# Two gates ahead of two values, and one output step fewer ahead of the first score burst: a change at the batch boundaries of an attention and gated feed-forward kernel

## The chip, the core and the metric

The kernel runs on one core of one Trainium2 chip. The metric is the device time of one execution in microseconds (us). The engines are named as the profile names them: PE (TensorE matmul), PEld (TensorE weight load), DVE (VectorE), ACT (ScalarE), POOL (GpSimd). The clock that PE was granted was 1.0 in the profiled executions.

## The reference, cut to what matters

```python
# 8 batches, 8 heads, 576 tokens, 16 beacon keys, head size 64
scores = scale * q @ k_all.T          # causal, the 16 beacon keys seen by all
a = softmax(scores)
x = (a @ v_all) as [4608 tokens, 512]
out = (gelu(x @ w_gate) * (x @ w_val)) @ w_out     # 512 -> 1536 -> 512
```

## The kernel before: the parts concerned

The feed-forward part runs in nine chunks of 512 tokens. For chunk b there are 12 gate/value tiles; each needs four gate matmuls, four value matmuls, a gelu on ACT and a product on DVE. The output matmuls of chunk b are delayed into batch b + 1, where they fill PE while ACT computes exponentials (at the boundary of batches 2 and 3 from 126.11 to 128.06 us, with exponentials on ACT from 125.97 on): a score burst fills one of three score buffers, and the exponential empties it. At each boundary the program has ACT load the function table for exp, 1.28 us in the trace, between the last gelu and the first exponential. Names with `psum` are the program's buffers for PE's results; a bank here is room for one 128x512 f32 tile. A half-height matmul is one that the profile shows as 64\*128 (a full one is 128\*128), and an output step of the first output tile is two of them side by side: in the trace of the kernel before, the two start 0.004 us apart (125.051 and 125.055) and the next step 0.216 us later (125.267).

```python
psum_s = ...bufs=3   # three buffers of two PSUM banks: scores, gate+value tiles, attention outputs
psum_t = ...bufs=1   # one bank
psum_o = ...bufs=1   # one bank

def gv_mms(ci, fi, *kks, split=False, last=False):
    # split: gate tile g_ps in psum_t, value tile v_ps in psum_s[:, 0]; else both in one psum_s buffer
    ...
    part(0)                       # the gate matmuls
    if not split: part(1)         # the value matmuls
    ...
    act(ge_sb, gv_of[ci, fi][0], ACT.Gelu)
    if split: part(1)
    ...
    keep(nc.vector.tensor_tensor(out=h_of[ci][:, fi, :], in0=gv_of.pop((ci, fi))[1], in1=ge_sb, op=ALU.mult))

def out_half_mms(ci, u0, u1):     # first output tile: two half-height matmuls side by side, one bank each
    for fi in range(u0, u1):
        if fi == 0:
            o_of[ci] = [..., (out_ps(0), out_ps(1))]          # psum_t and psum_o
        for g in range(2):
            r = slice(64 * g, 64 * g + 64)
            mm(halves[g], h_of[ci][r, fi, 0:P], wo_sb[r, fi, :], fi == 0, fi == F_TILES - 1, ...)
        if fi == F_TILES - 1:
            out_store(ci, 0, halves[0], o_half=halves[1])

def out_store(ci, ti, o_ps, c0=0, c1=D_MODEL, o_half=None):
    ...
        keep(nc.vector.tensor_copy(o_ap, o_half))                            # empties psum_o
        keep(nc.vector.tensor_tensor(out=o_ap, in0=o_ps, in1=o_ap, op=ALU.add))
    ...

for b in range(B):
    if b:
        keep(nc.scalar.preload_act_table_set(SET_EXP))
        o(3, b > 1)                       # b > 1: half height
        scores(b, (0, 0))                 # first burst: three buffers
        scores(b, (0, 2))
        scores(b, (0, 1))
        o(5 if b == 1 else 9, b > 1)      # the twelfth step ends the first output tile
        ...
        scores(b, (0, 3), (1, 3))         # fourth
        scores(b, (1, 0))
        scores(b, (1, 2))                 # needs the buffer of (0, 1): waits for the third exponential
        ...
        o(5 if b == 1 else 6)             # second output tile, full height, in psum_o
        ...
    for fi in range(F_TILES):
        if fi >= 2:
            gate_val(b, fi, fi == F_TILES - 1 and b < B - 1)
```

I count the score steps as the text does: (0, 0), (0, 2), (0, 1) are the first, second and third; (0, 3) with (1, 3) the fourth; (1, 0); and (1, 2), which the prediction calls the fifth burst.

The softmax here doesn't subtract the row's maximum and nothing guards it: scores larger than these inputs give would overflow.

## Time and profile before

| | before |
|---|---|
| median of 3 runs | 365.84 us |
| span of the profiled execution | 364.1 us |
| PE, ACT, DVE busy | 97%, 53%, 45% |
| one batch (start of the last product of a batch to the next) | 38.950 us, five times |
| PE's waits for exponentials | 0.9 us, 6 times |

The batch length is read from the trace as the distance between the starts of the DVE products that end each batch: 86.05 us for batch 1 and 280.80 for batch 6, so (280.80 - 86.05) / 5 = 38.95. The page's chain of waits by engine says which engines the end of the kernel hangs on:

```profile
span 364.1 us, 7726 instructions
PE 80%; DMA 8%; POOL 6%; ACT 3%; issue 2%; DVE 0%; ACTq 0%; POOLq 0%
```

The reader is to see ACT with 3%: the only engine besides PE that the chain meets in the steady batches. (DMA and POOL come in through the start-up: the chain's pieces from 80 to 174 us hold none of either.)

### The profile page before, as it was taken

Reading aid. Unit: us, or ns where it says so; the run is one execution under the profiler, and the core shown is the slowest. Engines: PE = TensorE matmul, PEld = TensorE weight load, DVE = VectorE, ACT = ScalarE, POOL = GpSimd, SP = SyncE. Lnnn points to the kernel's source line nnn. Section 1 sums busy time; section 2 is a strip of 40 time slices with the busy share of each in tenths; the row PEclk is TensorE's granted clock in tenths of the full one; section 3 lists DMA queues with packets and bytes.
Section 4 is the critical chain, followed back from the end, with each engine's and each line's share of the span. In section 5 each row is a group of like instructions: output and inputs, shape, how many; then the busy total and the mean of one; then the engine's idle time right before and its main releaser. Section 6 shows DMA issues by size and latency. Waiting matters only on the chain.

```text
span 364.1 us, 7726 instructions
## 1 busy us (share of the span) xinstructions
PE 353.7 (97%) x3164; PEld 184.8 (51%) x3206; DVE 162.8 (45%) x320; ACT 192.7 (53%) x252; POOL 161.2 (44%) x288
## 2 busy tenths in 40 slices
PE   7899999999999999999999999999999999999996
PEld 6665446444654455445644464446544564444443
DVE  4547836344443345434534354334444453333332
ACT  3975788237923594349623891379335953321210
POOL 8934497655537552945375455565330530000000
DMA  7999999899179945999299917991797253000102
GB/s 105 173 203 204 198 126 99 129 170 188 23 126 147 215 45 76 163 215 64 56 148 221 111 38 121 170 198 27 112 136 136 17 60 115 0 2 29 58 36 110
DMA packets 160419, 41.57 MB, mean 114 GB/s; under 512 B 146944, under 2 KB 155904, under 8 KB 160384
## 3 DMA queue, kind: packets, MB, share of 16 engines
q0 software_dynamic: 104848, 19.11, 68.9%
q1 hardware_dynamic: 55536, 21.96, 30.7%
q8 instruction: 25, 0.41, 0.5%
q14 instruction: 10, 0.08, 0.1%
HBM read 38.27 MB, written 9.44 MB: 131 GB/s over the span
## 4 chain that ended last, share of the span: by engine, by line
PE 80%; DMA 8%; POOL 6%; ACT 3%; issue 2%; DVE 0%; ACTq 0%; POOLq 0%
PE gv_ps L168 42%; PE o_ps L168 21%; PE x_ps L168 8%; PE s_ps L168 6%; DMA wo_sb<-in_moe_w_out_dram 4%; DMA qk<-in_q_dram 4%; ACT expT L171 3%; POOL qk L111 1%; PE g_ps L168 1%; PE v_ps L168 1%; POOL v_sb L111 1%; POOL q_sb L111 1%; POOL wg_sb L111 1%; POOL wv_sb L111 1%; POOL expT L320 1%
## 5 line engine op out<-in xcount | busy, mean ns | idle before, releaser
L171 ACT ACTIVATE ge_sb<-gv_ps 128x512 bf16<-128x512 f32 x101 | 59.4, 597 | 141.8 <-PE gv_ps L168 139.5
L448 DVE TENSOR_TENSOR hT_sb<-gv_ps,ge_sb 128x512 bf16<-128x512 f32 x101 | 69.0, 691 | 111.6 <-ACT ge_sb L171 109.2
L168 PE MATMUL gv_ps<-xT_sb,wg_sb 128*128 128x512 bf16 x402 | 111.2, 379 | 0.5
L168 PE MATMUL gv_ps<-xT_sb,wv_sb 128*128 128x512 bf16 x388 | 107.9, 379 | 0.4
L171 ACT ACTIVATE expT<-s_ps 128x992 bf16<-128x992 f32 (+3 forms) x112 | 100.2, 979 | 7.0 <-PE s_ps L168 6.4
L168 PE MATMUL o_ps<-wo_sb,hT_sb 128*128 128x512 bf16 (+3 forms) x492 | 101.0, 373 | 1.3
L320 POOL TENSOR_SCALAR_AFFINE_SELECT expT<-expT 128x256 bf16<-128x256 bf16 (+1 forms) x140 | 52.2, 391 | 51.2 <-ACT expT L171 50.0
L168 PEld LDWEIGHTS <-wv_sb 128*128 128x128 bf16 x432 | 42.3, 98 | 50.6
L168 PEld LDWEIGHTS <-wg_sb 128*128 128x128 bf16 x432 | 42.1, 98 | 49.9
L168 PEld LDWEIGHTS <-hT_sb 128*128 128x128 bf16 (+1 forms) x516 | 39.5, 97 | 42.4 <-issue 4.1
L168 PEld LDWEIGHTS <-expT 128*128 128x128 bf16 (+1 forms) x960 | 33.6, 97 | 10.0 <-DVE y_sb L356 3.1
L168 PE MATMUL x_ps<-v_sb,expT 128*128 128x65 bf16 (+1 forms) x960 | 37.4, 193 | 0.2 <-POOL expT L320 0.2
L168 PE MATMUL s_ps<-qkT 64*128 64x80 bf16 (+5 forms) x528 | 33.6, 250 | 3.4 <-DVE qkT L239 1.6
L111 POOL DMA_DIRECT2D v_sb<-in_v_dram x40 | 33.6, 859 | 6.0 <-DMA wg_sb<-in_moe_w_gate_dram 1.8
L111 POOL DMA_DIRECT2D k_sb<-in_k_dram x30 | 25.2, 844 | 15.4 <-DMA q_sb<-in_q_dram 10.8
L356 DVE TENSOR_TENSOR y_sb<-x_ps,r_sb 128x320 bf16<-128x320 f32 (+1 forms) x47 | 28.8, 612 | 1.6
L111 POOL DMA_DIRECT2D q_sb<-in_q_dram x30 | 25.3, 879 | 6.4 <-DMA wo_sb<-in_moe_w_out_dram 3.5
L469 DVE COPY o_sb<-o_ps 128x512 f32<-128x512 f32 (+2 forms) x31 | 20.7, 668 | 15.3 <-PE o_ps L168 14.2
L354 DVE RECIPROCAL r_sb<-x_ps 128x5 f32<-128x5 f32 (+1 forms) x47 | 9.6, 204 | 39.1 <-PE x_ps L168 39.1
L168 PEld LDWEIGHTS <-qkT 64*128 64x128 bf16 x528 | 18.1, 95 | 17.2 <-issue 8.9
L399 POOL COPY hold_sb<-xT_sb 128x2 bf16<-128x2 bf16 x6 | 1.1, 186 | 30.8 <-DMA xT_sb<-y_sb 30.8
L471 DVE COPY o_sb<-o_ps 128x512 f32<-128x512 f32 x6 | 4.1, 691 | 15.4 <-PE o_ps L168 15.4
(58 smaller groups left out, 137.9 us busy)
## 6 DMA issues: line engine op xcount, KB each, us to landing
out_dram<-o_sb SPq DMA_DIRECT2D x35, 256.0 KB, 7.0
v_sb<-in_v_dram POOLq DMA_DIRECT2D x24, 128.0 KB, 9.0
q_sb<-in_q_dram POOLq DMA_DIRECT2D x18, 128.0 KB, 12.2
k_sb<-in_k_dram POOLq DMA_DIRECT2D x18, 128.0 KB, 5.8
wo_sb<-in_moe_w_out_dram POOLq DMA_DIRECT2D x3, 512.0 KB, 14.4
wg_sb<-in_moe_w_gate_dram POOLq DMA_DIRECT2D x2, 512.0 KB, 11.9
wv_sb<-in_moe_w_val_dram POOLq DMA_DIRECT2D x2, 512.0 KB, 13.5
v_sb<-in_v_dram POOLq DMA_DIRECT2D x8, 112.0 KB, 5.4
```

What stands on the lines that cost most here:

```text
L111: keep(nc.gpsimd.dma_start(out=out_ap, in_=in_ap))
L168: keep(nc.tensor.matmul(out_ap, lhsT, rhs, start=start, stop=stop, **kw))
L171: keep(nc.scalar.activation(out_ap, in_ap, func, **kw))
L320: nc.gpsimd.affine_select(out=d, in_=d, pattern=[[0, 2], [1, n]], compare_op=ALU.is_ge, fill=0.0, base=0, channel_multiplier=-1,)
L354: keep(nc.vector.reciprocal(r, x[:, :, :, D:DV]))
L356: nc.vector.tensor_tensor(out=y_of[i][:, :, h0:h1, :].rearrange("p j b d -> p b j d"), in0=x[:, :, :, 0:D], in1=r.to_broadcast([P, h1 - h0 ...
L399: keep(nc.gpsimd.tensor_copy(hold_sb, x[:, 0 : S : S - 1]))
L448: nc.vector.tensor_tensor(out=h_of[ci][:, fi, :], in0=gv_of.pop((ci, fi))[1], in1=ge_sb, op=ALU.mult)
L469: keep(nc.vector.tensor_copy(o_ap, o_ps))
L471: keep(nc.vector.tensor_copy(o_ap, o_half))
```

## The change

Its intent: bring the first exponential of a batch forward. The last gelu, and so the table load, is to come earlier because both gates of the last two tiles run before both values; the first scores are to come earlier because one output step moves from before the first burst to after it.

```diff
+    def gates_first(ci, *fis):
+        ge_of = {}
+        for fi, (pool, tag) in zip(fis, ((psum_t, "t"), (psum_o, "o"))):
+            g_ps = pool.tile([P, CH], FP32, name="g_ps", tag=tag)
+            part(ci, fi, 0, g_ps)
+            ge_of[fi] = gelu(g_ps)
+        for fi in fis:
+            v_ps = psum_s.tile([P, 2, CH], FP32, name="v_ps", tag="s")[:, 0, :]
+            part(ci, fi, 1, v_ps)
+            gated(ci, fi, v_ps, ge_of[fi])
 ...
-            o(3, b > 1)
+            o(3 if b == 1 else 2, b > 1)
             scores(b, (0, 0))
             scores(b, (0, 2))
             scores(b, (0, 1))
-            o(5 if b == 1 else 9, b > 1)
+            o(5 if b == 1 else 10, b > 1)
 ...
         for fi in range(F_TILES):
-            if fi >= 2:
-                gate_val(b, fi, fi == F_TILES - 1 and b < B - 1)
+            if fi >= 2 and (fi < F_TILES - 2 or b in (0, B - 1)):
+                gate_val(b, fi, b == 0 and fi == F_TILES - 1)
+            if fi == F_TILES - 2 and 0 < b < B - 1:
+                gates_first(b, fi, fi + 1)
```

The rest of the diff (cut) only takes the old helper apart into `part`, `gelu` and `gated`.

More of the change, by code (lines that the diff above doesn't have):

```diff
@@ L411, with part @@
     gv_of = {}
-    def gv_mms(ci, fi, *kks, split=False, last=False):
-        if (ci, fi) not in gv_of:
-            if split:
-                gv_of[ci, fi] = (
-                    psum_t.tile([P, CH], FP32, name="g_ps", tag="t"),
-                    psum_s.tile([P, 2, CH], FP32, name="v_ps", tag="s")[:, 0, :],
-                )
-            else:
-                gv_ps = psum_s.tile([P, 2, CH], FP32, name="gv_ps", tag="s")
-                gv_of[ci, fi] = (gv_ps[:, 0, :], gv_ps[:, 1, :])
-        n0 = ci * CH
-        def part(w):
-            for kk in kks:
-                mm(
-                    gv_of[ci, fi][w],
-                    (wg_sb, wv_sb)[w][:, kk, fi * P : (fi + 1) * P],
-                    xT_sb[:, kk, n0 : n0 + CH],
-                    kk == 0,
-                    last and kk == kks[-1],
-                    skip_group_check=True,
-                )
-        part(0)
-        if not split:
-            part(1)
-        if not last:
-            return
+    def part(ci, fi, w, ps, kks=range(K_CHUNKS), last=True):
+        n0 = ci * CH
+        for kk in kks:
+            mm(
+                ps,
+                (wg_sb, wv_sb)[w][:, kk, fi * P : (fi + 1) * P],
+                xT_sb[:, kk, n0 : n0 + CH],
+                kk == 0,
+                last and kk == kks[-1],
+                skip_group_check=True,
+            )
@@ L441, in gv_mms, with gelu, gated @@
+    def gelu(g_ps):
         ge_sb = fpool.tile([P, CH], BF16, name="ge_sb", tag="ge_sb")
-        act(ge_sb, gv_of[ci, fi][0], ACT.Gelu)
-        if split:
-            part(1)
+        act(ge_sb, g_ps, ACT.Gelu)
+        return ge_sb
+    def gated(ci, fi, v_ps, ge_sb):
         if ci not in h_of:
             h_of[ci] = hpool.tile([P, F_TILES, CH], BF16, name="hT_sb", tag="hT_sb")
-        keep(
-            nc.vector.tensor_tensor(
-                out=h_of[ci][:, fi, :], in0=gv_of.pop((ci, fi))[1], in1=ge_sb, op=ALU.mult
-            )
-        )
@@ L453, in gate_val, with gv_mms @@
-    def gate_val(ci, fi, split=False):
-        gv_mms(ci, fi, *range(K_CHUNKS), split=split, last=True)
+        keep(nc.vector.tensor_tensor(out=h_of[ci][:, fi, :], in0=v_ps, in1=ge_sb, op=ALU.mult))
+    def gv_mms(ci, fi, *kks, last=False):
+        if (ci, fi) not in gv_of:
+            gv_of[ci, fi] = psum_s.tile([P, 2, CH], FP32, name="gv_ps", tag="s")
+        gv_ps = gv_of[ci, fi]
+        for w in range(2):
+            part(ci, fi, w, gv_ps[:, w, :], kks, last)
+        if last:
+            gated(ci, fi, gv_ps[:, 1, :], gelu(gv_ps[:, 0, :]))
@@ new lines, in gate_val @@
+    def gate_val(ci, fi, split=False):
+        if not split:
+            gv_mms(ci, fi, *range(K_CHUNKS), last=True)
+            return
+        g_ps = psum_t.tile([P, CH], FP32, name="g_ps", tag="t")
+        v_ps = psum_s.tile([P, 2, CH], FP32, name="v_ps", tag="s")[:, 0, :]
+        part(ci, fi, 0, g_ps)
+        ge_sb = gelu(g_ps)
+        part(ci, fi, 1, v_ps)
+        gated(ci, fi, v_ps, ge_sb)
+    def gates_first(ci, *fis):
+        ge_of = {}
+        for fi, (pool, tag) in zip(fis, ((psum_t, "t"), (psum_o, "o"))):
+            g_ps = pool.tile([P, CH], FP32, name="g_ps", tag=tag)
+            part(ci, fi, 0, g_ps)
+            ge_of[fi] = gelu(g_ps)
+        for fi in fis:
+            v_ps = psum_s.tile([P, 2, CH], FP32, name="v_ps", tag="s")[:, 0, :]
+            part(ci, fi, 1, v_ps)
+            gated(ci, fi, v_ps, ge_of[fi])
```

## The prediction

What the trace of the kernel before shows at this boundary, for the terms that the prediction uses:

- Matmuls of 512 columns follow one another after 0.216 us, while most of their records last 0.376 to 0.379 us, so a gap between records understates a stall. That fewer columns take less in proportion is an estimate that the trace bears out to 0.01 us: the next matmul starts 0.162 us after one of 384 columns (125.699 to 125.861; 0.162 in proportion), and the two 208-column chunks take 0.183 us (128.056 to 128.239; 0.176).
- The table load takes 1.283 us, and the first exponential starts 0.011 us after its end (125.964 to 125.975). An event semaphore stands ahead of that exponential (125.902) and another ahead of the last product (124.934).
- From half height to full height the next matmul starts 0.094 us later than that pace (128.987 due, 129.081), and from full to half 0.096 (124.729 due, 124.825).

> **What bounds the kernel now.** I read the page first: the engine shares, then the waits of the tensor engine, then the chain of waits, then the timeline of one batch boundary engine by engine. The shares and the wait list:
>
> ```profile
> PE 353.7 (97%) x3164; PEld 184.8 (51%) x3206; DVE 162.8 (45%) x320; ACT 192.7 (53%) x252; POOL 161.2 (44%) x288
> PE s_ps L168 <- ACT expT L171: 0.9, 6, 0.2
> ```
>
> PE is busy 97% of 364.1 us and every other engine about half. After the start-up the wait list of PE has one repeated entry: six waits, 0.9 us in all, of score matmuls for an exponential. The change touches six batch boundaries (batches 1 to 6 into 2 to 7), so these six waits are its target. The windows view agrees that each batch is a copy of the last: 38.95 us per batch, PE busy 38.52 in each of five windows. The chain of waits at the boundary of batches 2 and 3:
>
> ```profile
> 124.89 0.76 PE o_ps L168 x6
> 125.65 0.65 PE s_ps L168 x14
> 126.30 0.02 issue
> 126.32 0.02 ACTq L171
> 126.33 0.56 issue
> 126.89 1.84 ACT expT L171 x2
> 128.73 0.04 issue
> 128.78 0.37 PE s_ps L168 x4
> ```
>
> The reader is to see that the chain, on PE everywhere else in a batch, crosses over to ACT here for 2.4 us and comes back at 128.78. The timeline of the same stretch:
>
> ```profile
> 124.07 0.60 ACT L171 ACTIVATE ge_sb<-g_ps 128x512 bf16<-128x512 f32 x1 [0.27 <-PE g_ps L168]
> 124.68 1.28 ACT L616 ACT_TABLE_LOAD   x1
> 125.00 0.69 DVE L448 TENSOR_TENSOR hT_sb<-v_ps,ge_sb 128x512 bf16<-128x512 f32 x1 [0.48 <-PE v_ps L168]
> 125.48 0.80 PE L168 MATMUL s_ps<-qkT 64*128 64x512 bf16 x14
> 126.11 2.11 PE L168 MATMUL o_ps<-wo_sb,hT_sb 64*128 64x512 bf16 x18
> 127.72 1.00 ACT L171 ACTIVATE expT<-s_ps 128x992 bf16<-128x992 f32 x1
> 128.06 0.56 PE L168 MATMUL s_ps<-qkT 64*128 64x128 bf16 x10
> 128.26 0.69 DVE L471 COPY o_sb<-o_ps 128x512 f32<-128x512 f32 x1 [2.57 <-PE o_ps L168]
> 128.78 0.37 PE L168 MATMUL s_ps<-qkT 64*128 64x384 bf16 x4 [0.16 <-ACT expT L171]
> ```
>
> The last gelu ends at 124.67, the table load for the exponential at 125.96, the first exponential starts at 125.97, the third ends at 127.72 + 1.00 = 128.72 and frees the score buffer that the fifth burst (head pair 1, chunk 2) needs: it starts at 128.78. Then o matmuls of full height go on at 129.08.
>
> **How long PE really stands still.** The 0.16 us shown is measured from the end of a 0.38 us record, but four such matmuls in a row span 1.03 us, so one starts every (1.03 - 0.38) / 3 = 0.216 us. The second burst group began at 128.06 with two 208-column chunks (416/512 x 0.216 = 0.18) and one of 512 (0.216); the fifth burst could have started at 128.45. PE loses 128.78 - 128.45 = **0.32 us** per boundary, six times: 1.9 us is the most that the change can be after.
>
> [...]
>
> **The change part by part.** No arithmetic is added or taken away: the same matmuls, activations, products and table loads, in another order. What moves:
>
> (a) *Gates first.* The last two chunks run gate, value, gate, value on PE, 4 x 0.216 = 0.86 us each. Now both gates come first, so the last gelu is ready one block earlier: it starts at 124.07 - 0.86 = 123.20 and the table load ends at about 125.10 instead of 125.96. The gates take the two single-bank buffers, whose last readers (copies of the previous output) ended some 18 us before; no wait there. Both gelus end by 123.80, long before the first o matmul at 124.83 wants these buffers. The products of the values keep their order: the second-last a little later than before, the last unchanged at 125.00 to 125.69, because its value matmuls still end the block.
>
> (b) *One o matmul fewer ahead of the first burst.* An o step here is two half-height matmuls side by side: three steps take 125.48 - 124.83 = 0.65, so 0.216 us each. The first burst starts at 125.27 and its first chunk is done 0.216 sooner. In the kernel before, the data path and the table path to the first exponential end together: chunk done at 125.48 + 0.38 = 125.86, plus 0.11 for the event semaphore and start, gives 125.97; the table gives 125.96. So (a) alone or (b) alone buys nothing, and both together start the exponentials **0.21 us** sooner, now limited by (b). The third exponential ends at 128.51 and the fifth burst can start at 128.56 instead of 128.78. The step that was moved lies between the bursts now, so PE's own position there is unchanged (128.45).
>
> Up to here the sum is 6 x 0.21 = 1.3 us. But two more limits lie right behind.
>
> (c) *The copy of the half-height output.* After the fifth burst PE writes the second output tile into the buffer that the DVE copy at 128.26 empties. That copy follows the twelfth o step, which stays where it was on PE (the moved step only changes sides of the burst). It ends at 128.95; with the 0.06 us that DVE to PE takes (the trace shows 58 ns where score matmuls of batch 0 waited for DVE) the o matmul can't start before 129.01. It started at 129.08 now, set by the fifth burst (464/512 x 0.216 = 0.20) and 0.10 for going from half height to full height (the same 0.10 shows between the last value matmul, next start due at 124.73, and the first o at 124.83). So of the 0.21 us, **only 0.07 us** survives: the wait for ACT is replaced by a wait for DVE.
>
> (d) *The third chunk of the first burst waits for the last product.* The score buffers are a ring of three. The third burst chunk (head pair 0, chunk 1) takes the slot of the last value tile, which is free when the last product ends, 125.69 + 0.06 = 125.75. Before, that chunk started at 125.48 + 0.216 + 0.196 = 125.89, with 0.14 to spare. Now it wants 125.68 and has to wait about **0.07 us**. This delay goes through PE: the ten o steps after it, so the copy too, come 0.07 later: copy end 129.02, o at 129.08. That is exactly the old time.
>
> Sum: +0.21 from the exponentials, of which (c) leaves 0.07 and (d) takes 0.07 back. **Net about 0.00 us per boundary**, 0 to 0.4 us in all.
>
> **The rivals.**
> *Full gain*: (c) and (d) don't bind, 6 x 0.21 = 1.3 us, 364.5. For it speaks the wait list, which names only ACT; against it the end of the copy at 128.95, 0.07 before the slack is used up. I give it 7%.
> *Copy only*: (d) does not bind, because the product runs sooner or the slot is another; 6 x 0.07 = 0.4 us, 365.4. The product waits for the value matmuls, which end where they did, so I see no reason for it to move: 25%.
> *Both bind*: 365.84 - 0 to 0.1. My main reading: 60%.
> *Slower*: the new buffers or semaphores make PE stop in the dense gate stretch, or the wait at the third chunk is longer than 0.07; say 0.05 to 0.1 per boundary, 366.1 to 366.4. DVE is idle 2.57 us before the copy and PE reads nothing new, so 8%.
> Transfers play no part: PE waits for no DMA at these boundaries.
>
> **Range and chances.** 0.60 x 365.8 + 0.25 x 365.4 + 0.07 x 364.5 + 0.08 x 366.2 = 365.64; I take 365.7. The range 365.2 to 366.05 holds the main reading, the copy-only case and a small loss; the runs before lie within 0.06 us of each other, so the noise adds little. 2% would be 7.3 us, far over even the 1.9 us ceiling: faster 0.01, same 0.985, slower 0.005.
>
> **What would show it right or wrong.** In the changed kernel: the table load should start one gate block (0.86 us) sooner against the first o matmul (a); the first exponential should start about 0.21 us sooner, some 0.4 us after the start of the first burst, with ACT idle before it (b); the six waits of PE for the exponentials should be nearly gone (c); the first full-height o matmul should start 0.06 us after the end of the DVE copy (c); the third chunk should start 0.06 us after the end of the last product (d); and the batch should still take 38.88 to 38.95 us. The prediction is wrong if the batch is shorter by 0.2 us, which would say that (c) does not hold, or longer than 39.0, which would say that the new order has a wait that I did not see.

## The result, and the profile after

| | before | after |
|---|---|---|
| median of 6 runs of each | 365.81 us (365.51 to 366.57) | 365.72 us (365.19 to 366.86) |
| span of the profiled execution | 364.1 us | 363.7 us |
| one batch | 38.950 us | 38.937 us |

The ratio of the changed kernel to the kernel before is 1.000, with a 95% interval of 0.9983 to 1.0017. A ratio here is the mean time of one kernel's fast runs over that of the other's in the same rounds, so it is not quite the ratio of the medians above. The time is the same; so is the length of a batch, to 0.013 us.

The chain of waits by engine, from the page of the changed kernel, and the waits of PE after it:

```profile
span 363.7 us, 7774 instructions
PE 96%; DVE 3%; issue 0%; ACT 0%
```

```profile
PE s_ps L168 <- DVE qkT L239: 1.4, 3, 0.6
PE w_ps L168 <- DVE idle L80: 1.1, 1, 1.1
PE o_ps L168 <- DVE o_sb L481: 0.9, 6, 0.2
```

The six waits for ACT are gone, and in their place stand six waits for DVE of the same length: 0.9 us in all, 0.2 at most. This is what a replaced wait looks like. The shares of the chain are to be read with care: before, ACT's 3% were the exponentials (six times 1.84 us). They are gone, but of DVE's 3% only about 1% are the copies that stand there now (six times 0.70 us; the page's lines have "DVE o_sb L481 1%"). The rest of it, and the fall of DMA and POOL, is the start-up: in the first 50 us the chain goes through PE and DVE ("DVE qkT L235 1%") where it went through POOL and DMA before. The change does not touch that part. The chain in order of time at the boundary of batches 2 and 3 of the changed kernel (start, length, what):

```profile
122.74 1.73 PE v_ps L168 x8
124.46 0.54 PE o_ps L168 x4
125.00 0.71 PE s_ps L168 x14
125.71 2.17 PE o_ps L168 x20
127.88 0.02 issue
127.91 0.70 DVE o_sb L481
128.61 0.04 issue
128.65 1.46 PE o_ps L168 x6
```

Where the chain of the kernel before crossed to ACT, this one goes through the ten output steps, then through the DVE copy that empties the bank, then back to PE. The timeline of the changed kernel at the same place, first ACT, then DVE, then PE (start, length, engine, what, and in brackets the idle time before it):

```profile
122.77 0.60 ACT L171 ACTIVATE ge_sb<-g_ps 128x512 bf16<-128x512 f32 x1 [0.27 <-PE g_ps L168]
123.39 1.28 ACT L626 ACT_TABLE_LOAD   x1
125.32 3.69 ACT L171 ACTIVATE expT<-s_ps 128x1024 bf16<-128x1024 f32 x4 [0.65 <-PE s_ps L168]
...
124.57 0.69 DVE L433 TENSOR_TENSOR hT_sb<-v_ps,ge_sb 128x512 bf16<-128x512 f32 x1 [0.17 <-PE v_ps L168]
127.91 0.69 DVE L481 COPY o_sb<-o_ps 128x512 f32<-128x512 f32 x1 [2.64 <-PE o_ps L168]
...
128.65 0.59 PE L168 MATMUL o_ps<-wo_sb,hT_sb 128*128 128x512 bf16 x2 [0.16 <-DVE o_sb L481]
```

ACT now has 0.65 us of idle time between table load and first exponential, where it had 0.01 before: the table is no longer in the path. And PE goes on 0.05 us after the copy's end (127.91 + 0.69 = 128.60, start 128.65).

All traces can be laid on one another if times are counted from the start of the last value matmul of a batch (124.51 in the kernel before, 124.08 in the changed one). This table is worked out from the single instructions of the traces at the boundary of batches 2 and 3, in us from that point:

| | before | after |
|---|---|---|
| table load ends | 1.451 | 0.587 |
| first exponential starts | 1.462 | 1.234 |
| last product ends | 1.177 | 1.178 |
| third score step starts | 1.383 | 1.231 |
| third exponential ends | 4.210 | 3.982 |
| step (1, 2) starts | 4.262 | 4.033 |
| DVE copy ends | 4.440 | 4.512 |
| first full-height o matmul starts | 4.568 | 4.564 |

The exponentials run 0.228 us sooner, step (1, 2) 0.229 sooner, and the o matmul after it 0.004 sooner.

### The profile page after: what moved, and what is told of

It is laid out like the page before. It is cut to its first block, busy times and chain, and to the rows that moved or that the text cites. A ratio compares the mean times of both kernels' runs of the same rounds, so it can differ in the third digit from the quotient of the medians.

```text
span 363.7 us, 7774 instructions
## 1 busy us (share of the span) xinstructions
PE 356.0 (98%) x3206; PEld 186.8 (51%) x3206; DVE 163.0 (45%) x320; ACT 193.2 (53%) x252; POOL 161.2 (44%) x288
## 4 chain that ended last, share of the span: by engine, by line
PE 96%; DVE 3%; issue 0%; ACT 0%
PE gv_ps L168 45%; PE o_ps L168 26%; PE x_ps L168 9%; PE s_ps L168 6%; PE v_ps L168 3%; PE g_ps L168 3%; PE t_ps L176 2%; DVE qkT L235 1%; DVE o_sb L481 1%; PE w_ps L168 1%; PE y_ps L176 0%; ACT qkT L171 0%; DVE y_sb L356 0%; DVE o_sb L479 0%; DVE qkT L239 0%
## 5 line engine op out<-in xcount | busy, mean ns | idle before, releaser
L171 ACT ACTIVATE ge_sb<-gv_ps 128x512 bf16<-128x512 f32 x95 | 55.9, 597 | 135.3 <-PE gv_ps L168 134.1
L433 DVE TENSOR_TENSOR hT_sb<-gv_ps,ge_sb 128x512 bf16<-128x512 f32 x95 | 64.9, 691 | 105.4 <-ACT ge_sb L171 105.3
L168 PE MATMUL o_ps<-wo_sb,hT_sb 128*128 128x512 bf16 (+3 forms) x516 | 104.7, 373 | 0.9 <-DVE o_sb L481 0.9
L168 PE MATMUL gv_ps<-xT_sb,wg_sb 128*128 128x512 bf16 x380 | 105.4, 379 | 0.0
L168 PE MATMUL gv_ps<-xT_sb,wv_sb 128*128 128x512 bf16 x380 | 105.3, 379 | 0.0
L168 PEld LDWEIGHTS <-hT_sb 128*128 128x128 bf16 (+1 forms) x516 | 40.8, 96 | 42.5 <-issue 4.1
L433 DVE TENSOR_TENSOR hT_sb<-v_ps,ge_sb 128x512 bf16<-128x512 f32 x13 | 9.0, 692 | 9.5 <-PE v_ps L168 9.5
```

Of the source, the lines that this page charges most:

```text
L168: keep(nc.tensor.matmul(out_ap, lhsT, rhs, start=start, stop=stop, **kw))
L171: keep(nc.scalar.activation(out_ap, in_ap, func, **kw))
L433: keep(nc.vector.tensor_tensor(out=h_of[ci][:, fi, :], in0=v_ps, in1=ge_sb, op=ALU.mult))
```

## The experiments

The theory: the wait for the exponential was real, but behind it lie the DVE copy, which leaves 0.07 us at best, and, set off by the earlier burst, a wait of the third score step for the last product, which delays the copy by that same 0.07. The rivals: one part of the change alone does the work; the exponentials or PE's own work still fix the time; the savings are independent. The gauge is the batch length, in the table above to a few thousandths of a microsecond; the timed runs spread over 1 us and more and can't see it. Four of the experiments are one execution each; their clock was 0.999 or 1.0 and their five batches are equal to 0.01 us.

**The gates-first order alone.** The changed kernel with three and nine output steps again.

```diff
-            o(3 if b == 1 else 2, b > 1)
+            o(3, b > 1)
-            o(5 if b == 1 else 10, b > 1)
+            o(5 if b == 1 else 9, b > 1)
```

> Part (a) alone: gates first, but three o steps before the first score burst as in the kernel before. My theory (both paths to the first exponential tie in the kernel before): the table load starts 0.86 us sooner in the batch, the first exponential does not, because its scores end where they did; PE still waits 0.16 us (by the profile) for the exponential in the second burst, and the batch takes 38.95 us. Rival (the gelu and its table load were what held the exponentials back): first exponential sooner by up to 0.86 us, that wait gone, batch 38.88 or less.

The one look gave 365.84 us and a batch of 38.943. ACT's timeline in this run:

```profile
123.07 0.60 ACT L171 ACTIVATE ge_sb<-g_ps 128x512 bf16<-128x512 f32 x1 [0.27 <-PE g_ps L168]
123.69 1.28 ACT L626 ACT_TABLE_LOAD   x1
125.83 1.02 ACT L171 ACTIVATE expT<-s_ps 128x1024 bf16<-128x1024 f32 x1 [0.86 <-PE s_ps L168]
```

The table is ready 0.86 us before the first exponential, which then waits for its scores. In the common count (from the start of the last value matmul) the exponential starts at 1.450 instead of 1.462, so the table held it by 0.012 us and no more. PE's wait before step (1, 2) is 0.145 us by its records, against 0.156. The rival falls; part (a) alone is worth 0.007 us per batch.

**One output step fewer alone.** The kernel before with two and ten steps, in gate, value, gate, value order.

```diff
-            o(3, b > 1)
+            o(3 if b == 1 else 2, b > 1)
-            o(5 if b == 1 else 9, b > 1)
+            o(5 if b == 1 else 10, b > 1)
```

> Part (b) alone: two o steps before the first burst, but gate, value, gate, value order. My theory: scores are ready 0.21 us sooner but the table load ends where it did, so the first exponential starts where it did (ACT not idle before it), the wait of 0.16 us of PE for the exponential stays, the third chunk of the first burst waits some 0.06 us for the last product, the batch takes 38.95 us, at most 0.01 more. Rival (the scores were what held the exponentials back): first exponential 0.2 us sooner, batch 38.94 or less.

The one look gave 366.02 us and a batch of 38.950. ACT's timeline:

```profile
124.75 1.28 ACT L616 ACT_TABLE_LOAD   x1
126.05 1.02 ACT L171 ACTIVATE expT<-s_ps 128x1024 bf16<-128x1024 f32 x1
```

Here the first exponential follows the table load at once (124.75 + 1.28 = 126.03), at 1.463 in the common count, as before. The third score step, at 1.231, waits for the product, so the ten output steps come later and eat into the wait that follows: PE's gap before step (1, 2) is 0.079 us by its records, not the 0.16 that I had expected to stay. The step itself starts where it did (4.261 and 4.262), and the expected batch was met. So only both parts together start the exponentials sooner, and part (b) alone is worth nothing.

**One wait fewer ahead of the last product.** The last product waits for PE and for ACT, and in the trace one of the two waits is an instruction of its own, an event semaphore 0.065 us ahead of the product (124.506 and 124.571 in the changed kernel). A two-column copy on DVE that reads the second gelu first is to make that wait needless.

```diff
             ge_of[fi] = gelu(g_ps)
+        keep(nc.vector.tensor_copy(seen_sb, ge_of[fis[-1]][:, 0:2]))
         for fi in fis:
```

> The changed kernel plus a two-column VectorE copy that reads the second gelu before the two products, so that the last product has only PE to wait for and needs no event semaphore of 0.065 us ahead of it. My theory (d: the third chunk of the first burst waits for the last product): the last product starts about 0.065 us sooner after the value matmuls, the third chunk no longer waits, the ten o steps, the half-output copy and the full-height o matmul after it come 0.06 us sooner, batch 38.87 us instead of 38.94, about 0.4 us in the whole kernel. Rival (the copy alone, or the exponentials, fix the time): batch 38.94.

The batch took 38.863 us, the median of 4 runs was 365.41 us (ratio to the kernel before 0.9992, interval 0.9962 to 1.0021, too wide to see 0.5 us). DVE's timeline in this run; no event semaphore stands ahead of the two products now:

```profile
123.59 0.45 DVE L462 COPY seen_sb<-ge_sb 128x2 bf16<-128x2 bf16 x1 [1.03 <-ACT ge_sb L171]
124.69 0.69 DVE L434 TENSOR_TENSOR hT_sb<-v_ps,ge_sb 128x512 bf16<-128x512 f32 x1 [0.17 <-PE v_ps L168]
128.03 0.69 DVE L483 COPY o_sb<-o_ps 128x512 f32<-128x512 f32 x1 [2.64 <-PE o_ps L168]
```

In the common count the product starts at 0.416 instead of 0.486, ends at 1.108, the third step starts at 1.167, just where PE is ready for it, the copy ends at 4.443 instead of 4.512, and the o matmul follows at 4.495, still 0.052 after the copy. So the wait (d) is shown: taking it away moves what follows by 0.06 to 0.07 us (the third step by 0.064, the ten output steps by 0.061, the copy and the o matmul behind it by 0.069). The batch gains 0.074.

**A short copy.** The copy that frees the bank takes 128 of 512 columns (0.29 us in this run, 0.69 in the changed kernel); the remaining 384 columns lose half of their sum, so the result is wrong (relative error 0.21).

```diff
-            keep(nc.vector.tensor_copy(o_ap, o_half))
-            keep(nc.vector.tensor_tensor(out=o_ap, in0=o_ps, in1=o_ap, op=ALU.add))
+            keep(nc.vector.tensor_copy(o_ap[:, 0:128], o_half[:, 0:128]))
+            keep(nc.vector.tensor_tensor(out=o_ap[:, 0:128], in0=o_ps[:, 0:128], in1=o_ap[:, 0:128], op=ALU.add))
+            keep(nc.vector.tensor_copy(o_ap[:, 128:512], o_ps[:, 128:512]))
```

> The changed kernel with the first eviction of the half-height output cut from 512 to 128 columns (wrong result on purpose in 384 columns of the first 128 rows of a chunk), so that the buffer comes free about 0.4 us sooner. My theory (c: after the change PE waits there for the copy, and the exponentials would allow 0.23 us more): the wait of PE o_ps for DVE o_sb (0.9 us, six times) is gone, the full-height o matmul comes 0.2 to 0.23 us sooner, batch 38.71 to 38.74 us, 1.2 to 1.4 us in the whole kernel. Rival (the exponentials or PE's own work fix the time, the copy only happens to end last): batch 38.90 or more.

The chain at this boundary, in this run, runs on PE alone:

```profile
126.03 2.16 PE o_ps L168 x20
128.19 0.62 PE s_ps L168 x14
128.81 0.32 PE o_ps L168
```

The copy ends at 4.111 and the o matmul starts at 4.340 instead of 4.564: 0.224 us sooner, as expected. The median of 4 runs was 364.97 us, ratio 0.997 (0.9942 to 0.9998). Of the five batches two took 38.72 us, as expected; the others took 39.09, 38.70 and 38.80, so the mean is 38.80. At the end of the longest, a last product started 0.36 us late and the third score step with it, while POOL was issuing three key loads; I did not follow that up. (The batch after it, 38.70, is counted from that late product, so it is not a gain.) The change's own gain, then, was there to be had: the copy withholds it.

**Both taken away.** The two-column read and the short copy together (the diffs of the last two experiments; wrong).

> Both limits taken away at once: the two-column VectorE read of the second gelu and the 128-column first eviction (wrong result on purpose). My theory: once the copy is short, the exponentials hold the fifth score burst (third exponential ends 3.98 us after the start of the last value matmul, the burst may start at 4.03), so the two savings do not add: batch 38.72 us as with the short copy alone, and the fifth burst is delayed by about 0.06 us. Rival (independent savings): 38.65 us.

364.79 us, batch 38.729. The third step starts at 1.167, but step (1, 2) starts at 4.035, against 4.033 with the short copy alone: the third exponential ends at 3.983 in both. PE could have issued it 0.093 us sooner, where about 0.06 was expected (the pair before it started at 128.120 by the trace of this run, half-height pairs follow one another after 0.216, so it was due at 128.336 and started at 128.429). So the savings do not add; with the copy out of the way the exponentials are the bound again.

**The short copy in the kernel before.** The same edit in the old order.

> The kernel before with the first eviction cut to 128 columns (wrong result on purpose). My theory: in the kernel before the exponentials end the wait of PE and the copy has 0.07 us to spare, so nothing changes: batch 38.95 us, PE still waits 0.16 us (by the profile) for the exponential. Rival (the copy was a limit of its own before the change): batch 38.90 or less.

365.56 us, batch 38.950. PE's wait for ACT before step (1, 2) is still there, as its timeline in this run shows, and the o matmul starts at 4.569 (4.568 before):

```profile
128.32 0.38 PE L168 MATMUL s_ps<-qkT 64*128 64x384 bf16 x4 [0.15 <-ACT expT L171]
```

The same edit that is worth 0.21 us per undisturbed batch after the change is worth nothing before it. The copy was not a limit until the change made it one.

**The first output tile at full height.** A version with a right result: the tile fills one bank, the second tile's bank is empty from the start, and no copy stands before it.

```diff
-            o(3 if b == 1 else 2, b > 1)
+            o(3 if b == 1 else 2)
-            o(5 if b == 1 else 10, b > 1)
+            o(5 if b == 1 else 10)
```

> The changed kernel with the first output tile computed at full height into one buffer, so that the second tile's buffer is empty from the start and no copy stands before it (right result). Cost: two more changes between full and half height around the first burst, about 0.09 us each, less one ahead of the first o matmul. My theory: the wait for the copy is gone; the full-height o matmul after the fifth burst comes about 0.1 us sooner, batch 38.84 us (38.80 to 38.88), 0.6 us in the whole kernel. Rival (the height changes cost as much as the copy): 38.93 or more.

A miss in size. The batch took 38.91 us (four of five; the last 39.02), a gain of 0.03 and not 0.10. The wait for the copy is gone, and the o matmul follows the scores at 4.526, but that is only 0.038 before the changed kernel's 4.564. The two changes of height that I charged with 0.18 us cost 0.22: the ten output steps begin at 1.569 (1.444 in the changed kernel) and step (0, 3) at 3.823 (3.603). (The record of the first of the ten matmuls is missing from this trace; 1.569 is read from the weight load that follows its start, and the nine that are recorded fit it at 0.216 apart.) And the o matmul at 4.526 was followed by the next after 0.226 us instead of 0.216, which takes 0.01 more. Median of 4 runs 365.56 us, ratio 0.9984 (0.9968 to 1.0001).

**Full height and the two-column read.** Both edits, right result, the candidate.

> The full-height first tile and the two-column VectorE read together (right result): the candidate to beat both kernels. My theory: with no copy behind it PE sets the pace up to the fifth burst, so the 0.06 us of the third chunk add: batch 38.77 us (38.73 to 38.82), about 1.0 us less than the changed kernel, 364.7 us. Rival (the exponentials hold the fifth burst, no gain on top of the full-height tile): 38.84.

The batch took 38.84 us (four of five; the last 38.94), median of 6 runs 365.06 us, ratio 0.9982 (0.9959 to 1.0004). The expected 38.77 was missed, and 38.84 is the very number that the rival named. But the base was 38.91 and not 38.84, and against that base the point of the experiment held: here the 0.07 us of the product come through whole, because neither copy nor exponential stands behind them (step (1, 2) at 4.159 instead of 4.232). In the last batch ACT waited once for 0.5 us for POOL, and that batch is 0.1 us longer; the two go together in the repeat and in the full-height run before it as well (there 0.6 us and 0.11), but I have not shown that one causes the other.

**The changed kernel and the candidate once more, on one chip.**

> The changed kernel unaltered, timed beside the candidate on one chip, because its first six runs spread over 1.7 us. My theory: the batch is 38.94 us again and the time that of the kernel before less 0.1 us, so the interval holds 1.000. Rival (it gains or loses something that the batch length does not show): off by more than 0.5 us from the kernel before.

> The full-height first tile with the two-column read, once more, on the same chip as the changed kernel. My theory: batch 38.84 us, six times 0.11 less than before, so about 0.65 us below the kernel before and 0.55 below the changed kernel, with the ratio near 0.998. Rival (its first timing was luck of the chip): no difference, batch other than 38.84.

The changed kernel: median of 5 runs 365.79 us, batch 38.937, ratio 1.0005 (0.9991 to 1.0019); the kernel before, beside it, 365.81. The candidate: 365.30 us, batch 38.84 (the last again 38.94), ratio 0.9992 (0.9978 to 1.0005). Against the medians of before in the same job it is 0.87 us faster the first time and 0.51 the second; the expected ratio near 0.998 lies in the second interval, but the measured one is less than half as far from 1. The mean batch lengths agree to 0.001 us between the two jobs for both kernels. Over the five batches the candidate's trace is 0.45 us shorter than that of the kernel before (5 x 38.950 against 194.30) and 0.38 shorter than that of the changed kernel. Over these batches of the traces it beats both; by whole runs it is the same within the noise, as both intervals hold 1.

## Why the prediction was right, point by point

- *What bounds the kernel, and the 0.32 us lost per boundary.* Right in kind: from the full-height o matmul of one boundary to the last value matmul of the next, both kernels and all experiments take 34.37 to 34.39 us. The exceptions are the last batch with the short copy alone (34.46) and with the full height (34.49). The ceiling itself was not reached in any run.
- *(a) Gates first.* Right. The load ends at 0.587, 0.864 us sooner, and the new buffers cost no wait. Alone it gave 0.007 us per batch.
- *(b) One step fewer; both together start the exponentials 0.21 us sooner.* Right, 0.228. The claim that neither part alone buys anything was tested and held to 0.007 us. The "some 0.4 us" from the start of the first burst to the exponential was loose: the trace has 0.48 (0.753 to 1.234), and the prediction's own 0.38 and 0.11 make 0.49.
- *(c) The copy.* Right: six waits for ACT became six waits for DVE, and PE goes on 0.052 us after the copy (0.06 expected). The short copy showed that it is the copy that holds the o matmul, and the same edit in the kernel before showed that it was not a limit there.
- *(d) The third score step waits for the last product.* Right: without a wait it would start at 1.167, it starts at 1.231, which is 0.053 after the product's end. The wait is 0.064 us and (d) was put at 0.07. It doesn't appear in the list of waits, because the records of the matmuls before it cover it (they run to 125.416, and the step starts at 125.316); the experiment with the earlier product showed it.
- *The sum.* Put at 0.00 us per boundary, measured 0.013. The table and the records account for it: the o matmul starts 0.004 sooner, and the second matmul after it follows after 0.430 us and not after 0.443 (the record of the one between is missing in the kernel before). The 0.43 shows where this o matmul waited for the copy, the 0.44 where it followed the scores at once; that the wait is the reason is my reading of the records, not an experiment.
- *The central value.* 365.7 against 365.72 is luck at this precision: the runs spread over 1.7 us. The spread was under-sized; I took 0.06 us from three runs. In twelve profiled executions of all these kernels the first boundary (last product of batch 1) fell anywhere between 85.3 and 86.2 us, while the batches after it keep their length to about 0.01 us in most runs: in these executions most of the spread is made in the start-up, not where the change is.

## What to carry to other kernels

When a profile shows a single repeated wait, work out the next limit before taking the wait away: for each instruction behind it, when would its other inputs and its buffer be ready? Here the copy stood 0.07 us behind the exponentials, and the wait for the last product took even those 0.07. Taking the product's wait away gave 0.07 us per boundary; taking the copy's away let 0.22 of the 0.23 through, and the product's wait was then worth nothing more. And where one period repeats in a trace, compare the period: it resolved 0.01 us where whole runs could not resolve 0.5.

## What the traces showed of the hardware here

- Weight load and matmul pairs at 512 columns: in the dense gate and value stretch of the kernel before, one pair takes 215 or 216 ns.
- The table load: 1283 ns at the boundary of batches 2 and 3 of the kernel before; it starts 18 ns after the gelu's end, and the first exponential 11 ns after the load's end.
- The event semaphore ahead of the last DVE product: with the two-column read, the product came forward by 0.070 us (0.486 to 0.416).
- Going between half-height and full-height matmuls: 0.094 to 0.103 us beyond the pace of the matmuls, in either direction, in all 40 places of the kernel before from 80 to 280 us (0.09 to 0.11 in the full-height run). In the full-height run two more such changes put step (0, 3) 0.220 us later, which decided between two versions here. What takes this time is not shown.
